# State rows by batch then row on the partitions, and batch 3's x loaded and cast for its transpose before batch 4's

## The chip, the cores and the metric

One core of one Trainium2 chip runs the kernel. The metric is device time in microseconds (us), the median of the runs of one program. Engines are named as in the profile: PE (TensorE matmul), PEld (its weight load), DVE (VectorE), ACT (ScalarE), POOL (GpSimd), SP (SyncE, which only issues transfers here).

## The reference

x is (8, 8, 512, 64): batch, head, row, width. state is (8, 8, 32, 64). For each batch and head both sides read each other; the two results are stacked to 544 rows a batch, the heads are put side by side to 512 columns, and a two-matrix maxout layer follows.

```python
scores = scale * np.matmul(x, state.transpose(0, 1, 3, 2))
...
xread = np.matmul(a, state)          # a: softmax of scores over the 32 state rows
...
sread = np.matmul(a2, x)             # a2: softmax of the transposed scores over the 512 x rows
return np.concatenate([xread, sread], axis=2)
...
h1 = x @ w1
h2 = x @ w2
g = np.maximum(h1, h2)
return g @ w_out                     # w1, w2: 512 x 1024, w_out: 1024 x 512
```

The output has 4352 rows of 512 float32: for each batch 512 rows from x and then 32 rows from the state.

## The kernel before, in words

The maximum is written as relu(h1 - h2) + h2, so the kernel needs the difference of the first two matrices (`wd`) and the product of the second with the third (`wwo`), both made at the start. For the x rows a product with the state stands in front of both matrices, so the state is multiplied into them once per batch (`sw_mm`, L348, result tile `sw`).

The work is staged by batch. For a batch b: its x is loaded in two halves of four heads (`load_x`, L163, a 512 KB transfer each), cast to bf16 twice, once into `xe` in four pieces (`cast_e`, L230, 512 columns each) and once into `xb` in two pieces (`cast_b`, L234, 1024 columns each). `xb` is turned into x^T (`xt`) by a transposing transfer from SP (`xt_dma`, L238). `xe` is read later by the product that makes the state's reading (`sr_mm`, L296). From `xt` PE makes the scores (`sc_mm`, L255, matmuls at L261); ACT takes the exponential; DVE sums and inverts; POOL normalizes (`mul`, L276); a second transposing transfer makes `at` (`at_dma`, L281). The first layer (`l1_mm`, L374, matmuls at L377) reads `at` and `sw`, and its relu is split between ACT and DVE. The second layer is a scheme of seven half-size products (`product`, L425, matmuls at L428) with sums made on DVE (`r_sum`, L416) and a few extra terms (`opened`, L431, matmuls at L434), one of which reads a difference that POOL makes (`difference`, L421). `store` (L468) writes a batch's 512 rows: 128 partitions of 8 KB each for the middle batches.

PE works on batch b's first layer, then on the scores of batch b + 1, then on the second layer of b, interleaved with the state products of b + 1.

For batches 0 and 1, and for the start of 2 and 3, the order is written out by hand in a table of tokens (`ORDER`, L23 to L45). In it `ldx.3.0` is the load of the first half of x of batch 3, `ce.3.k` and `cb.3.k` are its casts to `xe` and `xb` (on POOL), `xtd.3` its transposing transfer, `atd.2` the transposing transfer of `at` for batch 2, `store.0` the store of batch 0, and `dif.1` the difference for batch 1. From L733 on a loop over b = 2 to 6 writes the order, and L818 to L870 write the last batch. Every transfer but one is issued by SP, in the order of the program; an SP instruction that waits holds all that are behind it.

The state rows take a path of their own: the reading of batch b is transposed (`sr_tr`, L336, matmul at L338) and ACT copies it into `sread_t` (`sr_cp`, L341), which holds all 256 state rows as columns, in two tiles t of 128 (t = b // 4). At the very end they go through the first layer (`m1`, L472, matmuls at L475) and a seven-product scheme of their own (`m_product`, L513, matmuls at L515 and L517), woven into the last batch. The results lie in `rs_o`, one state row to a partition, and `m_store` (L522) writes them in three transfers: columns 256 to 511 of tile 1 (128 KB, rows of 1 KB), the whole of tile 0 (256 KB, rows of 2 KB), and last of all columns 0 to 255 of tile 1 (128 KB). That last one, L870, is the last transfer of the kernel. Two stores of 256 KB for batch 7 (`store`, 128 partitions, two rows of 1 KB each) stand between the second and the third.

The order of a tile's 128 state rows is set in two places that must agree, `sr_cp` and `m_store`: with q = b % 4 and n the state row within a batch, the row is at n * 4 + q.

Of the kernel before, what the change touches and what calls it, by code (L numbers as in the profile page):

```python
# [35 lines left out]
sw.1.0@0,5 swe.0.0.0>A swe.0.0.1>V sw.0.w@1,3 sw.1.w@7,6 cb.2.1>P swe.1.0.0>A swe.1.0.1>V xtd.2 wt.1>P p2.1@2 l1.0.6@4  # L36
swe.0.w.0>A re.0.6>V l1.0.3@0 l1.0.2@5 swe.0.w.1>A re.0.3>V swe.1.w.0>V mS.1>A l1.0.1@4 l1.0.0@1 p2.0@3 swe.1.w.1>V
mS.0>A Sd dif.0>P re.0.2>V re.0.1>A re.0.0>A p2o.0 l1.1.0@7 l1.1.1@6 l1.1.2@0 l1.1.3@5 re.1.0>V re.1.1>A re.1.2>A
rs.0.0>V rs.0.1>V re.1.3>A p2o.1 ldx.4.1 ldx.3.0 ldx.4.0 ldx.3.1 p1.0@1 k0.0>A p1.1@4 rs.0.2>V wt.2>V v00.0 p6.0
rs.0.3>V k0.1>A k1.0>A p5.0@7 wt.3>V v00.1 rs.1.0>V k2.0>A sc.2.0@6 exp.2.0>A sc.2.1@0 exp.2.1>A sw.2.0@5,3 red.2.0>V  # L40
mul.2.0>P red.2.1>V swe.2.0.0>A swe.2.0.1>A ce.2.0>A ce.2.1>A ce.2.2>A ce.2.3>A p7.0 o7.0 v11.0 rs.1.1>V mul.2.1>P
p3.0 o3.0 rs.1.2>V atd.2 sw.2.w@6,2 swe.2.w.0>A v01.0 swe.2.w.1>A p4.0 o4.0 rs.1.3>V ce.3.0>P ce.3.1>P cb.3.0>P
ce.3.2>P ce.3.3>P cb.3.1>P v10.0>A store.0 xtd.3 dif.1>P sr.2@0 p6.1 k1.1>A sw.2.1@5,3 sre.2>V swe.2.1.0>A swe.2.1.1>V
p5.1@7 k2.1>A p7.1 o7.1 v11.1 p3.1 o3.1 v01.1 srt.2@0 srte.2>A p4.1 o4.1 v10.1>A ldx.5.0 ldx.5.1
"""  # L45

# [8 lines left out]
def kernel(  # L55
# [9 lines left out]
    nc = tc.nc  # L65
    B, H, S, D = x.shape
    _, _, Ns, _ = state.shape
    L = S + Ns
# [19 lines left out]
    def bank(ring="r", dtype=F32):  # L88
        if isinstance(ring, int):
            i = ring  # L90
        else:
            r = rings[ring]
            i = r[turn[ring] % len(r)]
            turn[ring] += 1
        return banks[i] if dtype == F32 else banks[i].bitcast(BF16)

    def copy(eng, o, i):
        if eng == "A":
            nc.scalar.copy(o, i)  # L99
        elif eng == "V":  # L100
            nc.vector.tensor_copy(o, i)  # L101
        else:
            nc.gpsimd.tensor_copy(o, i)  # L103

    def many(n, name, shape, dtype=BF16):
        return [sbuf.tile([128, *shape], dtype, name=f"{name}{i}") for i in range(n)]
# [8 lines left out]
    sread_t, = many(1, "sread_t", [4, NT])  # L115
# [33 lines left out]
    wt = big[3].bitcast(BF16).rearrange("p (k f n) -> p k f n", k=4, f=4)  # L149
    st = big[5].bitcast(BF16).rearrange("p (k f t) -> p k f t", k=4, f=4)  # L150
    part = big[6][:, 0:1536].rearrange("p (k n) -> p k n", k=3)
    dif = big[6][:, 1536:2048].bitcast(BF16).rearrange("p (z g n) -> p z g n", z=2, g=2)
# [119 lines left out]
    def red(b, hh):  # L272
        nc.vector.tensor_reduce(es_all[:, b, hh], e_view(e_s[b % 2], hh), axis=AXX, op=ALU.add)  # L273
        nc.vector.reciprocal(er_s[b % 2][:, hh], es_all[:, b, hh])
# [21 lines left out]
    def sr_mm(b, ring):  # L296
        p = bank(ring)
        for c in range(NC):
            for g in range(2):
                for k in range(4):  # L300
                    nc.tensor.matmul(p[32 * k:32 * k + 32, 65 * g:65 * g + 65], e_s[b % 2][:, g, c, k],
                                     xe_s[b % 3][:, c, k, 7 + 65 * g:72 + 65 * g],
                                     start=(c == 0 and g == 0), stop=(c == NC - 1 and g == 1), skip_group_check=True)
        return p

    def sr_ev(p, b):
        nc.vector.reciprocal(rr_all[:, b], p[:, 0:130:129])
        for g in range(2):
            nc.vector.tensor_scalar(sr_s[b % 2][:, g, :], p[:, 1 + 64 * g:65 + 64 * g],
                                    scalar1=rr_all[:, b, g:g + 1], scalar2=None, op0=ALU.mult)  # L310
# [29 lines left out]

    def sr_cp(p, b, eng):  # L341

        o = sread_t.rearrange("p k (t n q) -> p k t n q", t=2, q=4)
        copy(eng, o[:, :, b // 4, :, b % 4], p[:, 0:128].rearrange("p (k n) -> p k n", k=4))

    def sw_mm(b, lo, hi, rA="r", rB="r"):  # L348
        pg = [bank(rA), bank(rB)]
        n = hi - lo  # L350
        for i in range(4):
            for g in range(2):
                rhs = wd[64 * g:64 * g + 64, i, lo:hi] if hi <= FF else wwo[64 * g:64 * g + 64, i, lo - FF:hi - FF]
                nc.tensor.matmul(pg[g][32 * i:32 * i + 32, 0:n],  # L354
                                 sbd[64 * g:64 * g + 64, b, i, 32 * g:32 * g + 32], rhs, start=True, stop=True)
        return pg

    def sw_ev(pg, b, lo, hi, g, eng):
        copy(eng, sw_s[b % 3][:, g, lo:hi], pg[g][:, 0:hi - lo])
# [46 lines left out]
    def wq(j, k):  # L406
        return wo[:, 4 * j:4 * j + 4, 256 * k:256 * k + 256]

    def rq(b, i, j):
        return r_s[b % 2][:, 4 * j:4 * j + 4, 256 * i:256 * i + 256]  # L410
# [14 lines left out]
    def product(pv, lhs, rhs, first=False, cc=(0, 1)):  # L425
        for c in cc:
            for f in range(4):
                nc.tensor.matmul(pv[c], lhs[:, f, 128 * c:128 * c + 128], rhs[:, f, :],  # L428
                                 start=first and f == 0 and (c == 0 or pv.split), stop=False, skip_group_check=True)

    def opened(b, pv, i, rhs, cc=(0, 1)):  # L431
        for c in cc:
            for g in range(2):
                nc.tensor.matmul(pv[c], at_s[b % 3][:, g, 2 * i + c, :], rhs[:, g, :], start=False, stop=False,  # L434
                                 skip_group_check=True)
# [12 lines left out]
    def keep(k, pv, eng):  # L448
        if pv.split:
            for c in range(2):  # L450
                copy(eng[c], part[:, k, 256 * c:256 * c + 256], pv[c])
        else:
            copy(eng, part[:, k], pv.p[0])

    def put(b, i, k, pv, kept=None, eng="V"):
        for c in ((0, 1) if pv.split else (None,)):
            o = out_q(b, i, k) if c is None else out_q(b, i, k)[:, c]
            p = pv.p[0].rearrange("p (c n) -> p c n", c=2) if c is None else pv[c]
            if kept is None:
                copy(eng, o, p)  # L460
            else:
                u = part[:, kept].rearrange("p (c n) -> p c n", c=2)
                add("V", o, p, u if c is None else u[:, c])

    def so_half(b, k):
        return sw_s[b % 3][:, :, FF + 256 * k:FF + 256 * k + 256]
# [53 lines left out]
        return rs_o[:, t, 256 * k:256 * k + 256]  # L520

    def m_store(t, eng=None, lo=0, hi=DM):  # L522
        (eng or nc.sync).dma_start(out=out.rearrange("(t q l) m -> t l q m", t=2, l=L)[t, S:L, :, lo:hi],
                                   in_=rs_o[:, t, lo:hi])


# [85 lines left out]
    def fresh(kind, b, lhs, rhs, at):  # L612
        pairs[kind, b] = Pair(at)
        product(pairs[kind, b], lhs, rhs, True)

    def sw_range(b, z):
        if z == "w":
            return FF, WC
        return CHUNKS[b][z] if b < 2 else (512 * z, 512 * z + 512)

    mms = dict(
        S=s_mm, xt=xt_mm, sc=sc_mm, at=at_mm, sr=sr_mm, srw=srw_mm, srt=sr_tr, l1=l1_mm, w2=w2_mm,
        sw=lambda b, z, *rr: sw_mm(b, *sw_range(b, z), *rr))
    evs = dict(
        xte=("xt", xt_ev), exp=("sc", lambda p, b, h, e: sc_ev(p, b, h)), ate=("at", at_ev),
        sre=("sr", lambda p, b, e: sr_ev(p, b)), srte=("srt", sr_cp), re=("l1", l1_ev), w2e=("w2", w2_ev))
    oth = dict(
        swre=lambda b, g, e: srw_ev(done[f"srw.{b}"], b, g, e), srp=sr_pick, gate=gate,
        ldS=load_s, ldx=load_x, ldp=load_p, ldw2=lambda k: load_w(2, moe_w2, k), ldw1=lambda k: load_w(1, moe_w1, k), ldwo=load_wo,
        idle=idle, fill=lambda k, r: idle(1, r, 512 if k >= 100 else 256, k >= 200), cS=s_cast, mS=lambda z, e: s_mask(z, LATE, B, e), Sd=lambda: s_dma(LATE, B), ce=cast_e, cb=cast_b, xtd=xt_dma,  # L630
        atd=at_dma, red=lambda b, h, e: red(b, h), mul=mul, cw2=w2_cast, sub=w_sub, cwo=wo_cast, ww=ww_mm,
        wwe=lambda i, e: copy(e, wwo[:, i, :], open_[f"ww{i}"]),
        wt=w_sum, rs=r_sum, dif=difference,
        p1=lambda b, at: fresh("X", b, rq(b, 0, 0), wq(0, 0), at), p2=lambda b, at: fresh("Z", b, rq(b, 0, 1), wq(1, 0), at),
        p5=lambda b, at: fresh("Y", b, st[:, 0], wt[:, 0], at), p6=lambda b: product(pairs["X", b], st[:, 1], wt[:, 1]),
        p7=lambda b: product(pairs["X", b], st[:, 2], wt[:, 2]), p3=lambda b: product(pairs["Y", b], st[:, 3], wq(1, 1)),
        p4=lambda b: product(pairs["X", b], rq(b, 1, 1), wt[:, 3]),
        p2o=lambda b: opened(b, pairs["Z", b], 0, so_half(b, 0)), o7=lambda b: opened(b, pairs["X", b], 1, so_half(b, 1)),
        o3=lambda b: opened(b, pairs["Y", b], 0, so_half(b, 1)), o4=lambda b: opened(b, pairs["X", b], 1, dif[:, b % 2]),
        k0=lambda b, e: keep(0, pairs["X", b], e), k1=lambda b, e: keep(1, pairs["X", b], e),  # L640
        k2=lambda b, e: keep(2, pairs["Y", b], e), v00=lambda b: put(b, 0, 0, pairs["Z", b], 0),
        v11=lambda b: put(b, 1, 1, pairs["X", b], 2), v01=lambda b: put(b, 0, 1, pairs["Y", b], 1),
        v10=lambda b, e: put(b, 1, 0, pairs["X", b], None, e),
        Se=lambda lo, hi, j, e: s_ev(done[f"S.{lo}.{hi}"], lo, hi, j, e), store=store,
        swe=lambda b, z, g, e: sw_ev(done[f"sw.{b}.{z}"], b, *sw_range(b, z), g, e))
    done = {}
    for tok in ORDER.split():
        name, _, at_ = tok.partition("@")
        name, _, eng = name.partition(">")
# [86 lines left out]
    for b in range(2, B - 1):  # L736
        n = b + 1
# [55 lines left out]
        p = sr_mm(n, "r")  # L793
# [11 lines left out]
        if b < 4:  # L805
            sr_cp(sr_tr(b - 2, "r"), b - 2, "A")
        sr_cp(sr_tr(n, "r"), n, "A")
        put(b, 1, 0, pX, None, "A")
        if n == B - 1:
            for k in range(4):  # L810
                m_sum(k, aq, sst, "P")
            p = bank("r")
# [5 lines left out]
    b = B - 1  # L818
# [37 lines left out]
    m_product(mY, sst[:, 3], rst[:, 3], vq(1, 1), wq(1, 1))  # L856
    add("V", m_out(0, 1), mY, mk[:, 1])
    m_store(0)
    product(pY, st[:, 3], wq(1, 1))
    opened(b, pY, 0, so_half(b, 1))  # L860
# [46 lines left out]
```

## Time and profile before

| | |
|---|---|
| median of the runs | 144.87 us |
| the runs | 144.87, 231.15, 144.86 us |
| profiled execution | 144.49 us, span 142.7 us |
| TensorE clock granted | 1.00 |
| PE busy | 134.8 us (94% of the span) |
| DVE, ACT, POOL busy | 104.5, 88.2, 72.4 us |
| HBM read, written | 15.20 MB, 8.91 MB |

How to read it: the span is the time from the program's first instruction to its last in the one profiled execution; 144.49 - 142.7 = 1.8 us lie around it. Times in the timeline are microseconds from the start of the span. A row of the timeline gives start, length, engine, line, operation, tiles and count, and in brackets how long the engine had been idle before it and what ended that. `SPq` rows are SP issuing a transfer: their length is the issue and not the transfer. In a table of windows each row gives a stretch, busy time of each engine in it, the clock, and at its end the mean busy share of the core's 16 DMA engines and what they moved in GB/s. Matmul ends are modelled, so the start of the next group is the safer mark.

### The profile page before, as it was taken

To read this page: it belongs to the slowest core of one execution; us is meant where nothing else is said; L and a number is where in the kernel's file an instruction comes from. 1 tells how busy PE (TensorE), PEld (TensorE's weight loads), DVE (VectorE), ACT (ScalarE), POOL (GpSimd) and SP (SyncE) were. 2 spreads that over 40 slices of the span, in tenths; PEclk is the share of its full clock that TensorE was granted. 3 is DMA by queue.
4 is the path that set the end of the run, shared out by engine and by line. 5 is a ranking of instruction groups with operands and counts; after the bars stand their busy time and mean duration, and the time that the engine had idled before them with its cause. 6 is when DMAs were issued, how large, how long until landed. Compare 5 with 4: busy or idle time off the path is not lost.

```text
span 142.7 us, 3661 instructions
## 1 busy us (share of the span) xinstructions
PE 134.8 (94%) x1442; PEld 95.1 (67%) x1442; DVE 104.5 (73%) x193; ACT 88.2 (62%) x172; POOL 72.4 (51%) x99
## 2 busy tenths in 40 slices
PE   6897999999999998999999999999999999999980
PEld 2475735456887764786678577857876786788860
DVE  3489979778999947974898489569948986847420
ACT  4357969887599445674874769086737745753220
POOL 4147335099019992699079909963980544200000
PEclk9999999999999999999999999999999999999999
DMA  4999999945999889979936999659217041502073
GB/s 128 337 365 395 387 384 386 341 80 102 179 330 276 299 172 293 135 189 275 403 129 122 211 356 199 146 207 238 43 38 294 2 78 71 225 0 78 12 246 119
DMA packets 36453, 29.50 MB, mean 207 GB/s; under 512 B 22609, under 2 KB 32337, under 8 KB 35537
## 3 DMA queue, kind: packets, MB, share of 16 engines
q1 hardware_dynamic: 36160, 29.10, 72.1%
q8 instruction: 12, 0.20, 0.5%
q10 hardware_dynamic: 272, 0.13, 0.3%
q14 instruction: 9, 0.07, 0.1%
HBM read 15.20 MB, written 8.91 MB: 169 GB/s over the span
## 4 chain that ended last, share of the span: by engine, by line
PE 75%; DMA 8%; DVE 5%; POOL 5%; ACT 2%; issue 2%; SPq 0%; POOLq 0%; DVEq 0%
PE bank L428 28%; PE bank L377 16%; PE bank L434 8%; PE bank L608 5%; DMA xt<-xb 4%; DVE big L404 4%; PE bank L354 4%; DMA big<-in_x_dram 3%; PE bank L261 3%; PE bank L475 2%; PE bank L517 2%; POOL xe L103 2%; PE bank L323 1%; POOL xb L103 1%; PE bank L550 1%
## 5 line engine op out<-in xcount | busy, mean ns | idle before, releaser
L277 POOL TENSOR_TENSOR a<-e,er 128x512 bf16<-128x512 bf16 x14 | 17.2, 1235 | 28.3 <-ACT big L99 20.9
L372 DVE TENSOR_SCALAR r<-bank 128x512 bf16<-128x512 f32 x32 | 21.9, 690 | 13.0 <-PE bank L377 12.6
L99 ACT COPY big<-bank 128x512 f32<-128x512 f32 (+2 forms) x40 | 21.8, 551 | 13.2 <-PE bank L434 5.5
L377 PE MATMUL bank<-at,sw 128*128 128x512 bf16 x128 | 29.5, 379 | 0.2 <-DVE sw L101 0.2
L428 PEld LDWEIGHTS <-big 128*128 128x128 bf16 x256 | 23.8, 97 | 6.1 <-DVE big L404 1.7
L99 ACT CAST sw<-bank 128x512 bf16<-128x512 f32 x36 | 20.1, 609 | 6.0 <-PE bank L354 6.0
L428 PE MATMUL bank<-big,big 128*128 128x256 bf16 x192 | 23.1, 273 | 0.1
L404 DVE TENSOR_TENSOR big<-bank,big 128x512 f32<-128x512 f32 (+1 forms) x25 | 16.5, 663 | 8.2 <-PE bank L434 7.8
L377 PEld LDWEIGHTS <-sw 128*128 128x128 bf16 x128 | 12.2, 97 | 13.5 <-ACT sw L99 0.5
L370 ACT ACTIVATE r<-bank 128x512 bf16<-128x512 f32 x32 | 18.3, 596 | 4.1 <-PE bank L377 3.9
L428 PEld LDWEIGHTS <-r 128*128 128x128 bf16 x192 | 18.2, 98 | 2.7 <-issue 0.5
L103 POOL CAST xe<-big 128x512 bf16<-128x512 f32 x23 | 16.2, 736 | 6.4 <-DMA big<-in_x_dram 6.4
L428 PE MATMUL bank<-wo,r 128*128 128x256 bf16 x128 | 15.5, 273 | 0.0
L103 POOL CAST xb<-big 128x1024 bf16<-128x1024 f32 x12 | 12.2, 1035 | 4.7 <-DMA big<-in_x_dram 4.7
L434 PE MATMUL bank<-sw,at 128*128 128x256 bf16 x96 | 14.4, 273 | 0.0
L99 ACT COPY sread_t<-bank 128x128 bf16<-128x128 bf16 x8 | 3.2, 472 | 17.3 <-PE bank L338 14.0
L434 PEld LDWEIGHTS <-at 128*128 128x128 bf16 x128 | 12.5, 98 | 1.7
L404 DVE TENSOR_TENSOR big<-r 128x1024 bf16<-128x1024 bf16 x16 | 11.6, 723 | 0.6
L273 DVE TENSOR_REDUCE sums<-e 128x16 f32<-128x512 bf16 x16 | 10.8, 675 | 0.3 <-ACT e L269 0.2
L269 ACT ACTIVATE e<-bank 128x512 bf16<-128x512 f32 x16 | 8.9, 596 | 3.2 <-PE bank L261 2.8
L404 POOL TENSOR_TENSOR big<-sw 128x512 bf16<-128x512 bf16 x8 | 9.2, 1151 | 1.3 <-issue 1.3
L101 DVE CAST sw<-bank 128x512 bf16<-128x512 f32 x12 | 7.9, 682 | 1.1 <-PE bank L354 1.1
(100 smaller groups left out, 186.9 us busy)
## 6 DMA issues: line engine op xcount, KB each, us to landing
big<-in_x_dram SPq DMA_DIRECT2D x14, 512.0 KB, 6.7
out_dram<-big SPq DMA_DIRECT2D x7, 1024.0 KB, 4.5
big<-in_moe_w_dram SPq DMA_DIRECT2D x8, 512.0 KB, 11.3
big<-in_moe_w_out_dram SPq DMA_DIRECT2D x4, 512.0 KB, 10.9
big<-in_x_dram SPq DMA_DIRECT2D x1, 1024.0 KB, 6.8
out_dram<-big SPq DMA_DIRECT2D x4, 256.0 KB, 2.8
sf<-in_state_dram SPq DMA_DIRECT2D x1, 384.0 KB, 10.4
out_dram<-w2m SPq DMA_DIRECT2D x2, 128.0 KB, 2.5
```

Source lines behind the costliest of these rows:

```text
L99: nc.scalar.copy(o, i)
L101: nc.vector.tensor_copy(o, i)
L103: nc.gpsimd.tensor_copy(o, i)
L269: nc.scalar.activation(out=e_view(e_s[b % 2], hh).rearrange("p (g c) i n -> p g c (i n)", g=2), in_=p.rearrange("p (c g m) -> p g c m", c= ...
L273: nc.vector.tensor_reduce(es_all[:, b, hh], e_view(e_s[b % 2], hh), axis=AXX, op=ALU.add)
L277: (nc.gpsimd if eng == "P" else nc.vector).tensor_mul(e_view(a_s[b % 2], hh), e_view(e_s[b % 2], hh), er_s[b % 2][:, hh].unsqueeze(3).to_b ...
L370: nc.scalar.activation(out=o, in_=p, func=ACTF.Relu)
L372: nc.vector.tensor_scalar(o, p, scalar1=0.0, scalar2=None, op0=ALU.max)
L377: nc.tensor.matmul(p, sw_s[b % 3][:, g, f * 128:(f + 1) * 128], at_s[b % 3][:, g].rearrange("p c t -> p (c t)"), start=(g == 0), stop=(g = ...
L404: (nc.gpsimd if eng == "P" else nc.vector).tensor_tensor(o, i0, i1, op=op)
L428: nc.tensor.matmul(pv[c], lhs[:, f, 128 * c:128 * c + 128], rhs[:, f, :], start=first and f == 0 and (c == 0 or pv.split), stop=False, ski ...
L434: nc.tensor.matmul(pv[c], at_s[b % 3][:, g, 2 * i + c, :], rhs[:, g, :], start=False, stop=False, skip_group_check=True)
```

## The change

Three edits are made. Two are in the table of tokens: the two halves of x of batch 3 are loaded before those of batch 4, and of batch 3's casts the two that feed the transpose (`cb.3.0`, `cb.3.1`) come right behind the first `ce`, with the transposing transfer `xtd.3` behind them and so ahead of `store.0`. The third is the order of a tile's 128 state rows: q * 32 + n in place of n * 4 + q, in both places.

```diff
-rs.0.0>V rs.0.1>V re.1.3>A p2o.1 ldx.4.1 ldx.3.0 ldx.4.0 ldx.3.1 p1.0@1 k0.0>A p1.1@4 rs.0.2>V wt.2>V v00.0 p6.0
+rs.0.0>V rs.0.1>V re.1.3>A p2o.1 ldx.3.0 ldx.3.1 ldx.4.0 ldx.4.1 p1.0@1 k0.0>A p1.1@4 rs.0.2>V wt.2>V v00.0 p6.0
...
-p3.0 o3.0 rs.1.2>V atd.2 sw.2.w@6,2 swe.2.w.0>A v01.0 swe.2.w.1>A p4.0 o4.0 rs.1.3>V ce.3.0>P ce.3.1>P cb.3.0>P
-ce.3.2>P ce.3.3>P cb.3.1>P v10.0>A store.0 xtd.3 dif.1>P sr.2@0 p6.1 k1.1>A sw.2.1@5,3 sre.2>V swe.2.1.0>A swe.2.1.1>V
+p3.0 o3.0 rs.1.2>V atd.2 sw.2.w@6,2 swe.2.w.0>A v01.0 swe.2.w.1>A p4.0 o4.0 rs.1.3>V ce.3.0>P cb.3.0>P cb.3.1>P xtd.3
+ce.3.1>P ce.3.2>P ce.3.3>P v10.0>A store.0 dif.1>P sr.2@0 p6.1 k1.1>A sw.2.1@5,3 sre.2>V swe.2.1.0>A swe.2.1.1>V
...
     def sr_cp(p, b, eng):
 
-        o = sread_t.rearrange("p k (t n q) -> p k t n q", t=2, q=4)
-        copy(eng, o[:, :, b // 4, :, b % 4], p[:, 0:128].rearrange("p (k n) -> p k n", k=4))
+        o = sread_t.rearrange("p k (t q n) -> p k t q n", t=2, q=4)
+        copy(eng, o[:, :, b // 4, b % 4], p[:, 0:128].rearrange("p (k n) -> p k n", k=4))
...
     def m_store(t, eng=None, lo=0, hi=DM):
-        (eng or nc.sync).dma_start(out=out.rearrange("(t q l) m -> t l q m", t=2, l=L)[t, S:L, :, lo:hi],
+        (eng or nc.sync).dma_start(out=out.rearrange("(t q l) m -> t q l m", t=2, l=L)[t, :, S:L, lo:hi],
                                    in_=rs_o[:, t, lo:hi])
```

On PE, DVE and ACT the instructions stand in the same order as before. On POOL, around batch 3's casts (`big_118` holds its x; the row above and below them are batch 2's normalization and batch 1's difference):

```order
 L277 TENSOR_TENSOR a_93<-e_91,er_95 128x8x64 x2
-L103 CAST xe_84<-big_118 128x2x4x64 x2
-L103 CAST xb_90<-big_118 128x4x4x64
-L103 CAST xe_84<-big_118 128x2x4x64 x2
-L103 CAST xb_90<-big_118 128x4x4x64
+L103 CAST xe_84<-big_118 128x2x4x64
+L103 CAST xb_90<-big_118 128x4x4x64 x2
+L103 CAST xe_84<-big_118 128x2x4x64 x3
 L404 TENSOR_TENSOR big_115<-sw_103 128x512
```

The same six casts stand there; the second `xb` cast moved from the sixth place to the third.

On SP, between the loads of x for batches 3 (`big_118`) and 4 (`big_110`) and the loads for batch 5 (`big_113`); `xt_88` is batch 3's x^T, `big_109` batch 0's output:

```order
-L164 DMA big_110<-in_x_dram 128x4x256
-L164 DMA big_118<-in_x_dram 128x4x256
-L164 DMA big_110<-in_x_dram 128x4x256
-L164 DMA big_118<-in_x_dram 128x4x256
+L164 DMA big_118<-in_x_dram 128x4x256 x2
+L164 DMA big_110<-in_x_dram 128x4x256 x2
 L282 DMA_TRANSPOSE at_101<-a_93 128x8x128
+L239 DMA_TRANSPOSE xt_88<-xb_90 128x16x128
 L470 DMA out_dram<-big_109 128x2048
-L239 DMA_TRANSPOSE xt_88<-xb_90 128x16x128
 L164 DMA big_113<-in_x_dram 128x4x256 x2
```

The two halves of batch 3 moved up to the first two places, and the transposing transfer now stands ahead of the store of batch 0.

On SP at the end of the program, the last stores; the sizes are those of the side in memory, outermost axis first:

```order
 L470 DMA out_dram<-big_116 128x2x256 x2
-L523 DMA out_dram<-w2m_80 32x4x256
-L523 DMA out_dram<-w2m_80 32x4x512
+L523 DMA out_dram<-w2m_80 4x32x256
+L523 DMA out_dram<-w2m_80 4x32x512
 L470 DMA out_dram<-big_116 128x2x256 x2
-L523 DMA out_dram<-w2m_80 32x4x256
+L523 DMA out_dram<-w2m_80 4x32x256
```

The three stores of state rows stay where they were; their outermost axis in memory now counts 4 and not 32, and the number of rows and of bytes is the same.

## The prediction

> **What bounds the kernel now.** I read the chain of waits first, then PE's timeline around the one place where that chain leaves PE late, then PE's busy time behind it, and the end. The page gives the chain by line:
>
> ```profile
> PE 75%; DMA 8%; DVE 5%; POOL 5%; ACT 2%; issue 2%; SPq 0%; POOLq 0%; DVEq 0%
> PE bank L428 28%; PE bank L377 16%; PE bank L434 8%; PE bank L608 5%; DMA xt<-xb 4%; DVE big L404 4%; PE bank L354 4%; DMA big<-in_x_dram 3%; PE bank L261 3%; PE bank L475 2%; PE bank L517 2%; POOL xe L103 2%; PE bank L323 1%; POOL xb L103 1%; PE bank L550 1%
> ```
>
> PE carries three quarters. Of the rest, the transpose of x and the casts on POOL ahead of it are what this change touches. PE's timeline shows the wait (batch 3's scores, the second row) and beside it the same pair of groups one batch later, where nothing waits:
>
> ```profile
> 51.84 3.62 PE L377 MATMUL bank<-at,sw 128*128 128x512 bf16 x16
> 56.13 0.64 PE L261 MATMUL bank<-sbd,xt 128*128 128x64 bf16 x16 [0.67 <-DMA xt<-xb]
> ...
> 65.96 3.62 PE L377 MATMUL bank<-at,sw 128*128 128x512 bf16 x16
> 69.41 0.63 PE L261 MATMUL bank<-sbd,xt 128*128 128x64 bf16 x16
> ```
>
> From the start of the first layer to the start of the scores it is 69.41 - 65.96 = 3.45 us without a wait and 56.13 - 51.84 = 4.29 with it. So the wait costs 0.84 us, and PE wants x^T of batch 3 at 51.84 + 3.45 = 55.29. PE's own window behind it:
>
> ```profile
> 56.13:138.51 82.38, 82.37 (x954) 1.00 0.61 162
> ```
>
> PE is busy for 82.37 of 82.38 us at full clock. Whatever is saved ahead of 56.13 reaches the end whole, as long as no supplier falls behind. Behind 138.51 it is ACT's copy, the last store of state rows, and the end.
>
> **The casts and the transfer, moved forward.** SP and POOL in that stretch:
>
> ```profile
> 44.42 1.61 SPq L282 DMA_TRANSPOSE at<-a  x1
> 46.63 0.36 SPq L470 DMA_DIRECT2D out_dram<-big  x1
> 50.00 1.79 SPq L239 DMA_TRANSPOSE xt<-xb  x1
> 51.84 1.78 SPq L164 DMA_DIRECT2D big<-in_x_dram  x2
> 54.34 5.30 SPq L239 DMA_TRANSPOSE xt<-xb  x1
> ```
>
> ```profile
> 44.34 2.09 POOL L103 CAST xe<-big 128x512 bf16<-128x512 f32 x2
> 46.38 1.04 POOL L103 CAST xb<-big 128x1024 bf16<-128x1024 f32 x1
> 47.67 1.32 POOL L103 CAST xe<-big 128x512 bf16<-128x512 f32 x2 [0.25 <-DMA big<-in_x_dram]
> 48.94 1.03 POOL L103 CAST xb<-big 128x1024 bf16<-128x1024 f32 x1
> 49.94 1.15 POOL L404 TENSOR_TENSOR big<-sw 128x512 bf16<-128x512 bf16 x1
> ```
>
> The transfer is issued at 50.00, when the sixth cast is done (48.94 + 1.03). In the new order three casts stand ahead of it: 44.34 + 1.04 + 1.04 + 1.03 = 47.45. It is issued 2.5 us earlier. Its landing in this trace:
>
> ```profile
> L239 SPq DMA_TRANSPOSE xt<-xb x6: 1789/3391/6448, 32.6 to 94.1; - x6
> DMA to landing us min/median/max: 4.5/6.7/10.0
> ```
>
> ```profile
> 50.00 6.08 DMA xt<-xb
> ```
>
> This one took 6.1 us, as the row of the chain of waits says; with that, x^T is there at 53.5, 1.8 us before PE wants it. At the shortest (4.5) it is 52.0. At the longest (10.0) it would be 57.5 and the wait would stay; but transfers that long stand behind a store or loads, and now only batch 2's short transposing transfer and the end of batch 4's loads are ahead. I take the whole **0.84 us** off; the ends are 0 and 0.84, since PE has nothing more to give there.
>
> What is pushed back costs nothing, each with its cover. The store of batch 0 goes from 46.63 to behind the transfer's issue, 47.45 + 1.79 = 49.2; its buffer is next written by the load at 78.42. Batch 5's loads follow it at 49.6, before their 51.84. Batch 4's loads come second; their first reader is the cast at 52.29, and batch 3's halves, now first in SP's queue, come before the 0.25 us wait that POOL had on the second half. The difference on POOL stays behind the same six casts, so it ends no later than 49.94 + 1.15 = 51.09, and PE reads it at 51.40; if the casts stretched by more than 0.3 us, PE would lose the excess there.
>
> ```profile
> 51.40 0.60 PE L434 MATMUL bank<-big,at 128*128 128x256 bf16 x4
> ...
> 52.29 2.02 POOL L103 CAST xb<-big 128x1024 bf16<-128x1024 f32 x2
> ...
> 78.42 1.09 SPq L164 DMA_DIRECT2D big<-in_x_dram  x1
> ```
>
> **The copies of the state rows.** Eight copies on ACT now write 32 elements in a row and not every fourth element.
>
> ```profile
> L99 ACT COPY sread_t<-bank 128x128 bf16<-128x128 bf16 x8 | 3.2, 472 | 17.3 <-PE bank L338 14.0 <-PE bank L813 3.2
> L99 ACT COPY big<-bank 128x256 f32<-128x256 f32 x7 | 2.5, 373 | 7.8 <-PE bank L434 4.6 <-PE bank L428 1.9 <-PE bank L517 1.2
> ```
>
> A copy of twice the elements in a row takes 373 ns, so each may fall from 472 to 373 or less, at least 0.8 us of ACT in all. ACT had waited 17.3 us for PE ahead of these copies, and PE waits for nobody from 56.13 on: worth 0. Were it not hidden, it would be a gain.
>
> **The stores of the state rows** are where I expect the loss. The end of the timeline:
>
> ```profile
> 135.23 1.30 SPq L523 DMA_DIRECT2D out_dram<-w2m  x2
> 137.29 1.42 SPq L470 DMA_DIRECT2D out_dram<-big  x2
> 138.54 0.37 ACT L99 COPY w2m<-bank 128x256 f32<-128x256 f32 x1 [0.23 <-PE bank L517]
> 138.94 0.76 SPq L523 DMA_DIRECT2D out_dram<-w2m  x1
> ```
>
> ```profile
> L523 SPq DMA_DIRECT2D out_dram<-w2m x3: 539/653/759, 135.2 to 138.9; - x3
> DMA to landing us min/median/max: 2.2/2.8/2.8
> ```
>
> The last store lands at 138.94 + 2.8 = 141.7, and the span ends 1.0 us later. The last two columns of these windows are the share of 16 DMA engines and GB/s:
>
> ```profile
> 136.25:136.50 0.25, 0.25 (x5) 0.22 (x4) 0.00 (x0) 0.00 (x0) 0.00 (x0) 1.00 0.02 4
> 136.50:136.75 0.25, 0.25 (x5) 0.23 (x3) 0.18 (x1) 0.00 (x0) 0.00 (x0) 1.00 0.76 258
> 136.75:137.00 0.25, 0.25 (x5) 0.23 (x3) 0.25 (x1) 0.00 (x0) 0.00 (x0) 1.00 0.81 266
> ...
> 137.25:137.75 0.50, 0.50 (x7) 0.46 (x5) 0.01 (x1) 0.09 (x1) 0.00 (x0) 1.00 1.00 377
> ...
> 140.50:140.75 0.25, 0.00 (x0) 0.00 (x0) 0.00 (x0) 0.00 (x0) 0.00 (x0) 1.00 1.00 340
> 140.75:141.00 0.25, 0.00 (x0) 0.00 (x0) 0.00 (x0) 0.00 (x0) 0.00 (x0) 1.00 0.18 53
> 141.00:141.25 0.25, 0.00 (x0) 0.00 (x0) 0.00 (x0) 0.00 (x0) 0.00 (x0) 1.00 0.07 25
> ```
>
> The first store of state rows moves its 128 KB from 136.50 to 137.00 on nearly all engines and lands at 135.23 + 2.2 = 137.4, 0.4 us behind its last bytes. One busy engine moves 340 / 16 = 21.2 GB/s in rows of 1 KB and 377 / 16 = 23.6 GB/s in rows of 2 KB. The last window, a share of 0.07, is one engine of sixteen at work while fifteen are idle: an engine's part of a transfer is fixed beforehand and not handed on. So a transfer is cut when it is issued. The old one had 32 as outermost axis in memory and 128 partitions on the other side, and sixteen parts came of it; the new one has 4 there, with 128 on the other side.
>
> No row shows a transfer with a short outermost axis, so the cost has two ends. If the cut goes by the 128 partitions, nothing changes: 0. If it goes by the outermost axis, the store has four parts and runs on four engines. Each of these then has, from 136.5 on: 131,072 / 4 bytes at 21.2 (1.54 us), 262,144 / 4 at 23.6 (2.78), its sixteenth of the two stores of batch 7 that queue behind (262,144 / 16 at 21.2, 0.77 each), and the last store (1.54). That is 7.40 us, so 143.9, and landed 0.4 later at 144.3 in place of 141.7: **+2.6 us**. The last store's issue, 138.94, is then long past; the queue on four engines sets the end.
>
> I take the upper end. The parts must be the same on both sides of the copy, and of an outermost axis of 4 only four equal parts can be made; the instruction's axis is the one thing about these stores that changed. It is a choice of mechanism, not a reading, and I keep 0 for the range.
>
> A rule of the Trainium skill speaks to this: "DMA: Bandwidth & Descriptors", section "Why a DMA increments its semaphore by 16 and not by 1", says that the number of engines is the largest up to 16 that divides the slowest axis longer than one of both sides. By that rule the old stores get 16 and the new ones 4, and the sum is the upper one; the trace agrees for the old ones (a share of 0.76 and 0.81) and shows no case of the new.
>
> **The sum**, against the profiled execution: 144.49 - 0.84 + 2.6 = 146.25 us. The median of the runs lies 0.38 above the profiled execution (144.87), so I state 144.87 + 1.76 = **146.6 us**, 1.2% slower. A change of 2% (2.9 us) is about what a measurement of this kernel can tell from none.
>
> **The rivals.** *Sixteen engines still* (not slower). The cut goes by partitions, or the transfer is split before it is issued; the end keeps its shape and only the wait is gone: 144.87 - 0.84 = 144.0. For it: the source has 128 partitions in both programs. Against it: the parts are fixed, and four does not divide into sixteen. It decides as soon as the stores run on 16 engines; on eight it would be about half way, 145.
>
> *Four engines, and one of them held.* While the stores run, other queues fetch instructions (from the DMA queues between 137.0 and 138.9 us):
>
> ```profile
> q8 instruction: 1, 0.02, 3.1%
> q14 instruction: 1, 0.01, 1.1%
> ```
>
> 3.1% of 16 engines over 1.9 us are 0.031 x 16 x 1.9 = 0.9 us on one engine. Now that falls on one of many idle ones; if it falls on one of the four, the end moves by 0.9: 147.5. By place, four of sixteen.
>
> *The transfer does not come in time*: landing takes 8 us or more as elsewhere in the trace, or the three casts wait for data, and the wait of 0.84 us stays while the stores cost 2.6: 147.5. Against it: the 1.8 us of margin.
>
> **How the numbers follow.** Four engines, none held: 0.58; the sum's own uncertainty (the rates 20 to 23 GB/s, the 0.4 us) puts it between 146.0 and 147.1. Sixteen engines: 0.24. Four with one held: 0.12. The transfer late: 0.06. As the second has more than 0.2, the range must hold it: 143.8 to 147.7. Faster by over 2% (under 142.0) has no mechanism here: 0.01. Slower by over 2% (over 147.8) needs the held engine and more, or the last two cases together: 0.10. Within 2%: 0.89.
>
> **What would show it.** In the profile after: the transposing transfer of batch 3 issued near 47.5, no idle time in front of that batch's scores, and PE without a gap to about 137.7; then stores of state rows with a landing of 4 us and more, windows at the end with a share near 0.25, and a span of about 144.4. I am wrong on the stores if the share there stays near 0.8 and the last store lands in 2.8 us, and on the transfer if PE's scores still wait on it.

## The result, and the profile after

| | before | changed |
|---|---|---|
| median of the runs beside each other | 145.01 us | 149.61 us |
| ratio | | 1.0327, 95% interval 1.0306 to 1.0347 |
| span of the profiled execution | 142.7 us | 147.8 us |

The change makes the kernel 3.3% slower. It was forecast slower, at 146.6 us with a range to 147.7; the measured time lies above the range.

The first half went as described. PE's timeline of the changed kernel, batch 2's first layer and batch 3's scores, and the windows of PE from there to its end:

```profile
52.19 3.62 PE L377 MATMUL bank<-at,sw 128*128 128x512 bf16 x15
55.65 0.63 PE L261 MATMUL bank<-sbd,xt 128*128 128x64 bf16 x16
...
55.65:138.03 82.38, 82.10 (x950) 1.00 0.61 166
```

55.65 - 52.19 = 3.46 us, the distance without a wait, and no idle time is named in front of the scores. The stretch behind it lasts 82.38 us, as before (four of the 954 matmul records are missing here, which is the 0.28 us of "idle"). SP and POOL ahead of it:

```profile
48.68 1.85 SPq L239 DMA_TRANSPOSE xt<-xb  x1
50.63 1.02 SPq L470 DMA_DIRECT2D out_dram<-big  x1
51.70 1.60 SPq L164 DMA_DIRECT2D big<-in_x_dram  x2
```

```profile
44.69 1.08 POOL L103 CAST xe<-big 128x512 bf16<-128x512 f32 x1
45.72 2.94 POOL L103 CAST xb<-big 128x1024 bf16<-128x1024 f32 x2
48.60 1.73 POOL L103 CAST xe<-big 128x512 bf16<-128x512 f32 x3
```

The transfer left at 48.68, not at 47.45: all of this execution is 0.35 us later at this point (52.19 against 51.84), and the two casts took 1.47 us each, not 1.04. What was spent there came back in the three casts behind them (0.58 us each) and in the 0.25 us wait that is gone, so the difference ended at 51.45, no later than before if the 0.35 us are taken off. By the semaphore of the transfer, x^T was there at 53.0, 2.7 us before PE's scores.

PE ended at 138.5 before and at 138.0 now, and the loss is wholly behind that. The end of the timeline:

```profile
134.64 1.35 SPq L523 DMA_DIRECT2D out_dram<-w2m  x2
136.81 2.99 SPq L470 DMA_DIRECT2D out_dram<-big  x2
138.05 0.37 ACT L99 COPY w2m<-bank 128x256 f32<-128x256 f32 x1 [0.23 <-PE bank L517]
139.89 0.55 SPq L523 DMA_DIRECT2D out_dram<-w2m  x1
```

From the start of ACT's last copy to the end of the span it was 142.7 - 138.54 = 4.2 us, and is 147.8 - 138.05 = 9.7: **+5.6 us at the end, -0.84 at the scores**, and 0.35 from the loads at the start (the chain of this execution goes there through a wait for the weights, `DMA big<-in_moe_w_dram`, which the chain before lacks), which differ from one execution to the next: in the kernel with the old table (`rows_only` below) batch 2's first layer starts at 52.26, later than here. The sum is the 5.1 us between the spans. The windows of the changed kernel's end, with share of 16 DMA engines and GB/s in the last two columns:

```profile
136.00:137.00 1.00, 1.00 0.25 61
137.00:138.00 1.00, 1.00 0.47 104
138.00:139.00 1.00, 1.00 0.14 8
139.00:140.00 1.00, 1.00 0.85 168
...
143.00:144.00 1.00, 0.50 0.27 84
144.00:145.00 1.00, 0.50 0.21 76
145.00:146.00 1.00, 0.50 0.08 30
146.00:147.00 1.00, 0.50 0.04 12
```

Three things stand in them. From 136 on the share is 0.25: four engines carry the first store of state rows. From 138 to 139 nearly nothing moves, 8 GB/s, although four engines are not done; the prediction has no such second. And from 143 on four engines and then fewer (shares of 0.27, 0.21, 0.08 and 0.04) bring the rest in, while twelve are idle. (PE is done at 138.03; the clock of 0.50 in the last rows has no part in this.)

The copies of the state rows on ACT fell from 472 to 267 ns and changed nothing, as ACT waited 17.3 us ahead of them as before:

```profile
L99 ACT COPY sread_t<-bank 128x128 bf16<-128x128 bf16 x8 | 1.9, 267 | 17.3 <-PE bank L338 14.0
```

### The profile page after: what moved, and what is told of

Read it like the earlier page. It is cut to its first block, busy times and chain, and to the rows that moved or that the text cites. A ratio compares the mean times of both kernels' runs of the same rounds, so it can differ in the third digit from the quotient of the medians.

```text
span 147.8 us, 3651 instructions
## 1 busy us (share of the span) xinstructions
PE 132.4 (90%) x1432; PEld 93.7 (63%) x1442; DVE 103.8 (70%) x193; ACT 87.6 (59%) x172; POOL 72.6 (49%) x99
## 4 chain that ended last, share of the span: by engine, by line
PE 77%; DMA 13%; ACT 1%; SPq 1%; issue 1%; DVE 0%; ACTq 0%
PE bank L428 34%; PE bank L377 17%; PE bank L434 9%; DMA big<-in_moe_w_dram 8%; DMA big<-in_x_dram 5%; PE bank L354 4%; PE bank L475 2%; PE bank L608 2%; PE bank L517 2%; PE bank L261 2%; PE bank L301 1%; PE bank L515 1%; SPq L164 1%; ACT wb L99 1%; DVE w2m L101 0%
## 5 line engine op out<-in xcount | busy, mean ns | idle before, releaser
L277 POOL TENSOR_TENSOR a<-e,er 128x512 bf16<-128x512 bf16 x14 | 17.3, 1236 | 27.5 <-ACT big L99 16.3
L103 POOL CAST xe<-big 128x512 bf16<-128x512 f32 x23 | 15.6, 710 | 6.1 <-DMA big<-in_x_dram 6.1
L103 POOL CAST xb<-big 128x1024 bf16<-128x1024 f32 x12 | 13.1, 1112 | 4.7 <-DMA big<-in_x_dram 4.7
L99 ACT COPY sread_t<-bank 128x128 bf16<-128x128 bf16 x8 | 1.9, 267 | 17.3 <-PE bank L338 14.0
```

Source lines behind the costliest of these rows:

```text
L277: (nc.gpsimd if eng == "P" else nc.vector).tensor_mul(e_view(a_s[b % 2], hh), e_view(e_s[b % 2], hh), er_s[b % 2][:, hh].unsqueeze(3).to_b ...
```

## The experiments

The last column is the time from the start of ACT's last copy to the end of the span, in the profiled execution; it leaves the loads at the start out. `tile0_last` ran once and has no interval.

| kernel | median, us | ratio to before (95%) | end, us |
|---|---|---|---|
| before | 144.8 to 145.1 | 1 | 4.2 |
| changed | 149.61 | 1.0327 (1.0306 to 1.0347) | 9.7 |
| order_only | 143.95 | 0.9957 (0.9929 to 0.9985) | 4.4 |
| rows_only | 150.06 | 1.0378 (1.0330 to 1.0426) | 9.6 |
| eight_blocks | 145.13 | 1.0024 (1.0011 to 1.0037) | 5.2 |
| four_sends | 146.83 | 1.0138 (1.0122 to 1.0155) | 6.7 |
| act_queue_4 | 149.11 | 1.0286 (1.0248 to 1.0323) | 8.6 |
| act_queue_32 | 144.16 | 0.9946 (0.9921 to 0.9972) | 4.0 |
| tile0_new | 146.82 | 1.0122 (1.0089 to 1.0154) | 7.0 |
| tile1_new | 145.44 | 1.0029 (0.9989 to 1.0070) | 5.4 |
| half_rows | 147.90 | 1.0199 (1.0118 to 1.0280) | 7.9 |
| no_batch7 | 148.28 | 1.0223 (1.0143 to 1.0303) | 8.0 |
| tile0_last | 149.83, one run | | 9.8 |

### Which half costs, and is it the number of engines

The first, `order_only`, is the kernel before with the two edits of the table; `rows_only` is the kernel before with the two edits of the rows.

> The kernel before with the two edits of the table alone (loads and casts of batch 3 first, its transposing transfer ahead of batch 0's store); rows and stores of the state as before. Theory A (few engines: the whole loss is at the stores of the state rows, which run on only as many DMA engines as their outermost axis counts): 144.2 us, the kernel before less 0.84; no idle time on PE ahead of batch 3's scores. Theory B (row pattern: runs of 32 neighbouring rows are slow to write, whatever the engines): 144.2 too. Theory C (the moved transfer and loads lose time further on): 145 or more.

> The kernel before with the new order of the state rows alone; the table as before. A and B: all of the loss, 149.6 + 0.84 = 150.4 us, and the last store landing some 8 us behind PE's end. C: 147 or less, since the table is the old one.

The other two keep both edits of the table and write the state rows in other ways.

```diff
 # eight_blocks: a tile holds 16 rows of each of the eight batches
-        o = sread_t.rearrange("p k (t q n) -> p k t q n", t=2, q=4)
-        copy(eng, o[:, :, b // 4, b % 4], p[:, 0:128].rearrange("p (k n) -> p k n", k=4))
+        o = sread_t.rearrange("p k (t q n) -> p k t q n", t=2, q=8)
+        copy(eng, o[:, :, :, b], p[:, 0:128].rearrange("p (k t n) -> p k t n", k=4, t=2))
...
-        (eng or nc.sync).dma_start(out=out.rearrange("(t q l) m -> t q l m", t=2, l=L)[t, :, S:L, lo:hi],
+        (eng or nc.sync).dma_start(out=out.rearrange("(q l) m -> q l m", l=L)[:, S + 16 * t:S + 16 * t + 16, lo:hi],
```

> The table of the change, and a third order of the state rows: a tile holds 16 rows of each of the eight batches, batch by batch, so that the outermost axis of the stores counts 8 and not 4. A: eight engines, half the backlog on each; the queue of stores is nearly done when the last is issued, so 144.6 to 145.7 us, a share of DMA engines near 0.5 while a store of state rows runs, and eight increments of its semaphore by transfers. B: runs of 16 rows, so half of the loss or more: 147 us or more.

```diff
 # four_sends
-        (eng or nc.sync).dma_start(out=out.rearrange("(t q l) m -> t q l m", t=2, l=L)[t, :, S:L, lo:hi],
-                                   in_=rs_o[:, t, lo:hi])
+        rows = out.rearrange("(t q l) m -> t q l m", t=2, l=L)
+        for q in range(4):
+            (eng or nc.sync).dma_start(out=rows[t, q, S:L, lo:hi], in_=rs_o[32 * q:32 * q + 32, t, lo:hi])
```

> The changed kernel with each store of state rows sent as four, one for each batch of the tile: the same rows from the same partitions to the same places, but 32 is the outermost axis of each. A: sixteen engines again; only the added issues cost, at the end three more of 0.4 to 0.55 us: 145.4 to 146.0 us. B: the pattern is the same, so about 149.6 us.

`order_only` is faster than before (143.95 against 144.76), `rows_only` carries the whole loss, and PE's wait is in the trace of the second and not in that of the first:

```profile
52.26 3.62 PE L377 MATMUL bank<-at,sw 128*128 128x512 bf16 x16
56.42 0.64 PE L261 MATMUL bank<-sbd,xt 128*128 128x64 bf16 x16 [0.54 <-DMA xt<-xb]
```

```profile
52.25 3.62 PE L377 MATMUL bank<-at,sw 128*128 128x512 bf16 x16
55.71 0.63 PE L261 MATMUL bank<-sbd,xt 128*128 128x64 bf16 x16
```

So C falls, and `order_only` beats both kernels of the study. `four_sends` writes the same rows from the same partitions to the same places and ends 3 us earlier than the changed kernel; its time is above A's 145.4 to 146.0, because SP issues eight transfers, 4.48 us in all, ahead of batch 7's last two stores, and A's sum had counted only the last four:

```profile
134.89 4.48 SPq L525 DMA_DIRECT2D out_dram<-w2m  x8
139.47 1.03 SPq L470 DMA_DIRECT2D out_dram<-big  x2
140.59 1.85 SPq L525 DMA_DIRECT2D out_dram<-w2m  x4
```

With eight blocks the end takes 0.8 us more than with 32 (5.2 against 4.4 in `order_only`) and 4.5 less than with four. A holds, and B falls. The trace shows the count directly: the semaphore of each store of state rows gets 16 increments from transfers in the kernel before; in the changed kernel it gets five, one about 1 us after the issue and four when the data land, and with eight blocks nine. The section of the Trainium skill that the prediction named ("DMA: Bandwidth & Descriptors", section "Why a DMA increments its semaphore by 16 and not by 1") says that the k engines of a transfer post one increment each and that the issuing sequencer writes the rest at once. The trace agrees, with the one extra increment about 1 us after the issue.

### Where the other 3 us come from

The backlog on four engines (the rows queued on each of them) was worth 2.6 us by the prediction, and the end of the kernel became 5.6 us longer. The first thought was SP: its second store in the window above took 1.95 us to issue, and the last store left at 139.89, 1.5 us behind ACT's copy.

```diff
 # act_queue_4, in the changed kernel; act_queue_32, in order_only
-    m_store(1, None, 256, 512)
+    m_store(1, nc.scalar, 256, 512)
...
-    m_store(0)
+    m_store(0, nc.scalar)
...
-    m_store(1, None, 0, 256)
+    m_store(1, nc.scalar, 0, 256)
```

> The changed kernel with its three stores of state rows issued by ACT and not by SP; four engines each as before. Theory D (the few engines' full queues hold SP, so that the two stores of batch 7 and the last store are late, and the engines stand idle meanwhile): the backlog alone is left on the four, 7.4 us from 136.0, that is 2.3 us more than with the table's edits alone: 146.3 us; the last store is issued right behind ACT's last copy. Theory E (the four engines themselves are slow or held, by the fetches of instructions among others; the queue is not at fault): 148.5 us or more, close to the changed kernel's 149.6.

> The control: the kernel with the table's edits alone and the old order of the state rows, and the three stores of state rows issued by ACT. D and E: as with SP's queue, 144.0 us, within 0.5.

The last store now leaves right behind the copy:

```profile
138.56 0.37 ACT L99 COPY w2m<-bank 128x256 f32<-128x256 f32 x1 [0.23 <-PE bank L517]
138.96 0.55 ACTq L523 DMA_DIRECT2D out_dram<-w2m  x1
```

and the kernel is 0.6 us faster than the changed one by the ratios (1.0286 against 1.0327, with intervals that overlap), not 3; the control, `act_queue_32`, came out at 144.16 us, as with SP's queue. D falls as the main cause; the engines themselves are slow, as E says. Which store makes them slow:

```diff
 # tile0_new and tile1_new, in order_only: the new row order in tile 0 alone, or in tile 1 alone
+        new = b // 4 == 0        # tile1_new: == 1
+        o = sread_t.rearrange("p k (t q n) -> p k t q n" if new else "p k (t n q) -> p k t q n", t=2, q=4)
```

(and the store of that tile alone as in the changed kernel).

> The table's edits, and the new order of state rows in tile 0 alone: only the 256 KB store in the middle runs on four engines. By the backlog alone it ends 0.5 us later than with the table's edits alone: 144.5 us. D: SP is held behind it, but less is queued on the four engines ahead of it: 145 to 146. E: the held engine adds 1 to 2 us: 145.5 to 146.5.

> The table's edits, and the new order of state rows in tile 1 alone: the first and the last store (128 KB each) run on four engines, the 256 KB store on sixteen. By the backlog alone: the last store lasts 1.54 us and not 0.39, and starts when it did: about 1 us more than with the table's edits alone, 145.0. D: 32 of the first store's rows per engine don't fill a queue that takes two such stores, so no more than that. E: 146 or more.

Against `order_only`, tile 1 costs 1.0 us (1.0029 - 0.9957, of 145) and tile 0 2.4. Tile 1 came out as its backlog, within an interval of 0.6 us to either side; tile 0, with only one store on four engines and a backlog of 0.5, costs more than twice as much as the two stores of tile 1, and its 146.82 us lie above what each of the theories gave it. So most of what is missing is in the 256 KB store with rows of 2 KB. Three kernels and one more transfer take it apart:

```diff
 # half_rows, in the changed kernel
-    m_store(0)
+    m_store(0, None, 0, 256)
+    m_store(0, None, 256, 512)
 # tile0_last, in the changed kernel: m_store(0) behind m_store(1, None, 0, 256)
 # no_batch7, in the changed kernel
-    store(b, 0, 2, 256, 512)
...
-    store(b, 2, 4, 0, 256)
 # early_copy, in order_only, behind the first store of batch 7
+    nc.sync.dma_start(out=out.rearrange("(t q l) m -> t q l m", t=2, l=L)[0, :, S:L], in_=ob(6)[:, 0])
```

> The changed kernel with tile 0's 256 KB store sent as two of 128 KB, each of half rows of 1 KB, still on four engines. Theory F (a store of 2 KB rows on few engines stands still for about 1.2 us after its first rows, by itself): the standstill is gone, 148.4 us or less. Theory G (the fetch of instructions that falls on that time holds the engines): no difference, 149.6 us. Theory H (the stores on sixteen engines that queue behind crowd the four): 149.6 us too.

> The changed kernel with tile 0's store issued last of all. F: the standstill goes with it, to the end of the run. G: it stays near 137.2 to 139, where the 16 KB fetch is. H: with one store less ahead of them, batch 7's stores run at their pace and no standstill is seen. The time alone tells nothing, about 149.5 us in all cases, 148.5 by H.

> The changed kernel without the last two stores of batch 7 (256 KB each; a quarter of that batch's rows each is not written), so that only the three stores of state rows are in the queue at the end. The four engines have 5.86 us of rows from 136.0 on. H: nothing else holds them: landed at 142.3, 145.1 us. F or G: 1.2 us later, 146.3 us.

> The kernel with the table's edits alone, and one transfer more, in the quiet time of the DMA engines near 130: 128 rows of 2 KB of an older result to the places of tile 0's state rows, with 4 as outermost axis (the right rows are written over them later). With 1.3 us from issue to the first row, 2.8 us of rows on four engines and 0.4 to land, it should land 4.5 us after its issue. G and H: it does, since there is neither a fetch nor another store. F: 5.7 us, with the slow rows at its start.

`half_rows`, with the same bytes on the same four engines in rows of 1 KB, takes 1.8 us off the end (7.9 against 9.7), and the second of 8 GB/s is gone. From 138 to 138.5, where the changed kernel moves 6 GB/s, it moves 92 on four engines:

```profile
138.00:138.50 0.50, 1.00 0.27 92
```

Its last store leaves on time too (138.36, 0.4 us behind the start of ACT's last copy), so the 1.8 us include whatever SP's late store cost. `no_batch7` has nothing behind the state rows and still stands still (16 GB/s and less from 138 to 139); it came out above what F and G gave it (148.28 against 146.3): H falls. In `tile0_last` (one run) the slow rows go to the end with the store, behind all others; its windows there:

```profile
142.00:143.00 1.00, 0.50 0.16 29
143.00:144.00 1.00, 0.50 0.21 47
144.00:145.00 1.00, 0.50 0.24 82
```

And `early_copy` shows it in a quiet time (its own 144.48 us, in one run, say nothing). Its transfer is issued at 129.02 and lands at 135.1 by the trace, 6.1 us and not 4.5. The DMA queues between 130.9 and 134 hold nothing else, no fetch among them:

```profile
DMA packets 95, 0.19 MB, mean 62 GB/s; under 512 B 1, under 2 KB 1, under 8 KB 95
...
q1 hardware_dynamic: 95, 0.19, 23.0%
```

so G falls, and F stands. Three of its windows:

```profile
130.75:131.25 0.50, 1.00 0.26 12
131.25:131.75 0.50, 1.00 0.18 12
...
132.75:133.25 0.50, 1.00 0.25 98
```

By the share, three to four engines are at work all along (0.18 to 0.26 of sixteen), but for a microsecond they move 12 GB/s, and only 2 us after the start of the first of these windows the 98 that they can.

### What makes the slow start

The last four put such a transfer, and nothing else, into the quiet time between 123 and 129, each changed in one respect; `quiet_half` halves the length of the rows and with it the bytes.

```diff
 # quiet_near, in order_only, ahead of the last batch's second layer; X is batch 7's 512 rows of the output
+    nc.sync.dma_start(out=X.rearrange("(g l) m -> g l m", g=4)[:, 0:32],
+                      in_=rs_r.rearrange("p f t -> p (f t)")[:, 0:1024].bitcast(F32))
 # quiet_apart: [:, 0:96:3]
 # quiet_half:  [:, 0:32, 0:256], and half of the source's columns
 # quiet_16:    g=16, [:, 0:8]
```

> The kernel with the table's edits alone and one transfer more while the DMA engines are quiet (near 125 to 129): 128 rows of 2 KB in four blocks of 32 neighbouring rows, the blocks 128 rows apart, into batch 7's place of the output, where the right rows are written later. The share of four engines alone: landed 4.5 us after its issue. Theory F1 (the store is slow to start because each engine writes rows that lie one behind the other): 5.5 us or more, with the standstill. Theory F2 (the cause is not the rows in memory but that 256 KB are handed to four engines): also 5.5 or more. Theory F3 (it is the distance of 544 rows between the four blocks): 4.5.

> The same, with the 32 rows of a block three rows apart. F1: no standstill, 4.5 us. F2: as with neighbouring rows, 5.5 us or more. F3: 4.5.

> The same blocks of 32 neighbouring rows, but half rows of 1 KB, 128 KB in all. By four engines alone: 1.3 + 1.54 + 0.4 = 3.2 us. F1: slow too, 4 us or more. F2: little or nothing, below 3.8. F3: 3.2.

> The control: the same 128 rows of 2 KB in sixteen blocks of 8 neighbouring rows. All theories: sixteen engines, 1.3 + 0.7 + 0.4 = 2.4 us, no standstill.

Their times say nothing (144.6, 145.1, 144.1 and 144.5 us, one run each). From issue to landing by the trace: near 5.9 us, apart 5.9, half rows 3.4, sixteen blocks 2.9. The windows, first of `quiet_near` (issued at 124.63), then of `quiet_apart` (125.05), of `quiet_half` (123.34), and of `quiet_16` (124.5):

```profile
125.80:126.30 0.50, 1.00 0.31 45
126.30:126.80 0.50, 1.00 0.26 12
126.80:127.30 0.50, 1.00 0.16 8
127.30:127.80 0.50, 1.00 0.17 49
```

```profile
126.25:126.75 0.50, 1.00 0.32 45
126.75:127.25 0.50, 1.00 0.27 12
127.25:127.75 0.50, 1.00 0.16 8
```

```profile
124.50:125.00 0.50, 1.00 0.20 29
125.00:125.50 0.50, 1.00 0.22 70
125.50:126.00 0.50, 1.00 0.27 96
```

```profile
125.65:126.15 0.50, 1.00 0.78 156
126.15:126.65 0.50, 1.00 0.84 225
126.65:127.15 0.50, 1.00 0.39 143
```

Rows three apart start just as neighbouring rows do, so F1 falls; blocks 128 rows apart start as slowly as blocks 544 apart, so F3 falls. What is left is F2: 128 rows of 2 KB in one transfer on four engines. Half rows start with little delay, and sixteen engines have a trace of it (156 GB/s in the first half microsecond, 0.5 us more than the 2.4 expected). The delay sits in the first rows. Between 125.9 and 127.38 `quiet_near` moves sixteen of its 128, four to an engine, with four engines busy (24.9% of sixteen); at the later 98 GB/s these 32 KB would take 0.33 us:

```profile
DMA packets 16, 0.03 MB, mean 22 GB/s; under 512 B 0, under 2 KB 0, under 8 KB 16
...
q1 hardware_dynamic: 16, 0.03, 24.9%
```

`quiet_half` moves its first sixteen between 124.6 and 125.12:

```profile
DMA packets 16, 0.02 MB, mean 32 GB/s; under 512 B 0, under 2 KB 16, under 8 KB 16
...
q1 hardware_dynamic: 16, 0.02, 21.8%
```

No run separates the length of the rows from the bytes of a transfer: `half_rows` and `quiet_half` change both, as each of their transfers has 128 KB. Why a transfer of 2 KB rows on few engines starts like that was not found.

## Why the prediction was right and wrong, point by point

*PE's wait, 0.84 us off*: right in its place, and its size is borne out by the trace. `order_only` has no wait, and it is 0.6 us faster by the ratio (0.43%, between 0.15 and 0.71%, that is 0.2 to 1.0 us). The time of issue was wrong by 0.9 us after the start's 0.35 is taken off, since the prediction gave each kind of cast one price. A cast has none: before, an `xe` piece took 1.04 us at 44.34 and 0.66 at 47.67, and the two `xb` casts, 1.04 and 1.03 in their old places, took 2.94 together in the new ones. What sets it was not tested. The margin covered it, with some luck: the transfer then landed 4.3 us after its issue, below even the 4.5 that the prediction had as the shortest.

*What is pushed back costs nothing*, and *the copies are worth 0*: right. PE's stretch behind the scores is 82.38 us in all three profiles.

*The choice of four engines against sixteen*: right. Eight blocks gave eight engines, and 145.1 us where the prediction had put eight at 145.

*The cost of the four engines, +2.6 us*: this is the term that failed; it measured +5.6. The step was "Each of these then has, from 136.5 on" so many bytes at 21.2 and 23.6 GB/s: it took the rates of engines that are at full pace and had them at that pace from the first row. Once running they are faster than that: 98 GB/s on four engines is 24.5 each, in `early_copy` with rows of 2 KB, and the 96 of `quiet_half` are 24 each with rows of 1 KB. In place of the term the runs show three parts. The backlog is real: `tile1_new`, which has rows of 1 KB alone on four engines, came out at its backlog. The start of the 2 KB store adds 1.4 to 1.6 us by itself in a quiet time, and `half_rows`, without it, is 1.8 us shorter at the end.

The rest, 1.2 to 1.6 us by difference, is not settled by any run, but the trace shows where it lies. By the prediction's sum, with 1.27 us from the issue to the first row as before (135.23 to 136.50), the last store of the changed kernel would land at 134.64 + 1.27 + 7.40 + 0.4 = 143.7. Its four increments are at 144.9, 145.1, 145.6 and 146.9: three engines are 1.2 to 1.9 us late, about the slow start, and one is another 1.3 us behind. That engine was behind at the end of the 2 KB store already (142.1, 142.3, 142.4 and 144.3), so the last store did not cause it, nor need the stores of batch 7: in `no_batch7` the same store's increments are at 142.1, 142.1, 143.0 and 143.6. What holds that engine is open.

*"The queue on four engines sets the end"*: right; the last store left 1.5 us behind ACT's copy and, put on time, gave back about 0.6 us by the ratios (`act_queue_4`).

*The rival with an engine held by a fetch of instructions* gave 147.5 and was nearer to the result than the forecast, but not by its mechanism as far as the standstill goes: that came in `early_copy` with no fetch beside it, and on all four engines at once. Whether a fetch held the one engine that ended last, no run shows.

*The range*: its upper end took in one held engine, and no mechanism by which all four are slow; a time over 147.8 us, which came, had 0.10. The cost came from a situation that no row of the trace before showed, a transfer on few engines, and its bounds were worked out from rows of transfers on sixteen.

## What to carry to other kernels

The order in which a store's axes are written decides how many engines carry it: here an outermost axis of 32 gave sixteen, 8 gave eight and 4 gave four, with the same rows and bytes; a shorter copy into the tile (472 to 267 ns, hidden) is no reason to give that up on the last store of a kernel. Where a transfer goes onto few engines, bytes at full pace give a lower bound for its time (2.6 us here, where 5.6 came), and the range should be left open upward. An early supplier is worth at most the wait that it removes: 0.84 us by the trace here, 0.6 by the times, and it is kept by taking the table's edits alone.

## What the runs showed of the hardware that was not expected

- A transfer of 128 rows of 2 KB on four engines moved 12 GB/s for about a microsecond at its start, with the engines counted as busy, and 98 GB/s later; with rows of 1 KB it was at 70 in the second half microsecond. Its first sixteen rows took 1.5 us, those of 1 KB 0.5.
- The semaphore of a transfer on four engines gets five increments and not sixteen, the first about 1 us after the issue; the profile then gives no time to landing for it.
- Two casts of 1,024 columns on POOL took 2.94 us at 45.7 and 2.02 at 52.65 in the same kernel, the changed one. A DVE sum of 128 x 1,024 beside the first pair took 0.92 us; before, it took 1.48 beside a cast of 1.04. What sets these times no run shows.
